# Hash attention beside an FFN on one core: the two casts of P ahead of the exponential, a hash's bits behind the gate's low part

## The chip, the core and the metric

The kernel runs as one program on one NeuronCore of a Trainium2 chip. The metric is the device time of one execution in microseconds (us); lower is better. Before the change the median of three runs is 974.77 us (974.68 to 978.98). Engines are named as in the profile: PE is TensorE, with PEld for its weight loads, DVE is VectorE, ACT is ScalarE, POOL is GpSimd, SP is SyncE, which here only issues DMAs.

## The reference

Four batches of eight heads, 768 tokens, head width 64. Each token's query and key are hashed to a six-bit bucket by the signs of six projections; a query attends only to keys of its own bucket. The result goes through a feed-forward network (FFN) with 512 inputs, 2048 hidden units and a gate. All is float32; the FFN's weights come as 64-bit floats.

```python
q_bits = (np.einsum('bhsd,dk->bhsk', q, proj) > 0).astype(np.int64)
...
mask = q_bucket[:, :, :, None] == k_bucket[:, :, None, :]
scores = scale * np.matmul(q, k.transpose(0, 1, 3, 2))
scores = np.where(mask, scores, -1000000000.0)
scores = scores - np.max(scores, axis=-1, keepdims=True)
attn = np.exp(scores)
attn = attn / (np.sum(attn, axis=-1, keepdims=True) + 1e-09)
return np.matmul(attn, v).astype(np.float32)
...
h = x @ w_in
relu6 = np.clip(h + 3.0, 0.0, 6.0)
g = h * relu6 / 6.0
return (g @ w_out).astype(np.float32)
```

## The kernel before

**Splitting.** Nearly every matrix product is made of three fp32r products: each operand is a high part (a cast on ACT) and a low part (the difference, on DVE or POOL), and the product of two low parts is left out. So each operand costs a cast and a subtraction, here called `ph` and `pl` for the attention matrix P, `gh` and `gl` for the gate's output (tiles `gb` and `ga`).

**Steps.** The attention is cut into 192 steps, six tiles of 128 queries for each of 32 heads. What a step `g` needs, in order: scores on PE (`s`, lines 387 and 389); their lowest value and a copy out of PSUM on DVE (`lowest`, line 396); the exponential on ACT, in place (line 408); P turned over; the cast and the low part of P (`split_p`, lines 475, 477 and 479); and, for each pair of steps, the product with the values on PE (`acc`, lines 500 and 513).

**The stage of the change.** From step 102 (`GT`) on the attention runs beside the FFN: `beside_ffn(k)` writes down, for each step `k`, one slice of attention and one of 16 slices of an FFN chunk of 256 tokens. The orders on PE, DVE, ACT and POOL are the orders in which this function calls things; SP's queue is ordered by the scheduler. In this stage P is turned over by a DVE transpose of 32 x 32 blocks (`flip`, line 429), one DMA to DRAM (`fd`) and four DMAs back (`move`), which end in one of two tiles, `spare` for even steps and `px` for odd ones. Flip(k+2) and move(k+1) belong to step k; a move is issued behind the next flip's write to DRAM, and only when the two casts and the two low parts of the same tile's last content are done. The casts of step k are those of P(k-1), in two halves: half 1 (its low part on POOL, line 477) and half 0 (its low part on DVE, line 479). `ph` and `pl` have two buffers each, so one pair of steps fills both, and the cast of the next pair must find them free.

**The FFN's slice.** `gemm1` (12 matmuls, line 661) gives h; `gate` is a Relu on ACT (line 683) and a multiplication on DVE (line 684); at the next step's start `split_g` casts `gh` on ACT (line 689) and subtracts `gl` on DVE (line 690); `gemm2` (lines 699, 700 and 704, the last with `gl`) runs after the next step's `gemm1`. In this stage `gh` and `gl` have one buffer, so a cast waits until the `gemm2` before it has read it. The generator `ffn` yields at stages A to D, and `go("A")` and so on in `beside_ffn` run it up to the next.

**One step's order before the change.** PE: `acc` (odd steps), `gemm1`, the hash `z` (one step in six, lines 334 to 336), `gemm2` of the last slice, the scores of step k+3. ACT: `gh`, exponential, cast of half 1, on odd steps a copy `y` of a product (line 547), Relu, cast of half 0, on some steps a scaling (line 274) or cast (line 304) of the next head's q and k. DVE: `lowest`, `gl`, `flip`, gate, `pl` of half 0, and on a hash's step `bits` (line 352, two instructions), which turns `z` into the bit rows of q, from where a DMA copies rows to k; the scores of the next head need them two steps later. On the step behind a hash `gl` stands ahead of `lowest`. `add` lets POOL issue DMAs that accumulate the second half of a head's result into DRAM (`xs`).

Of the kernel before, what the change touches and what calls it, by code (L numbers as in the profile page):

```python
# [28 lines left out]
LA = 3  # L29
# [3 lines left out]
LT = 1  # L33
# [10 lines left out]
def lsh_attention_moe(  # L44
# [10 lines left out]
    nc = tc.nc  # L55
# [3 lines left out]
    KT = S // P  # L59
# [20 lines left out]
    paced = False  # L80
# [147 lines left out]
    NS = NJ * KT  # L228
# [3 lines left out]
    GT = GF + FT  # L232
# [139 lines left out]
    scs, probs, outs = {}, {}, {}  # L372
# [110 lines left out]
    def split_lows():  # L483
        for f in lows:
            f()
        lows.clear()
# [31 lines left out]
    adds, fresh = [], []  # L518
# [10 lines left out]
    def output(un: int):  # L529
        nonlocal vdone  # L530
        i, u = divmod(un, KT // 2)
        b, h = divmod(i, H)
        o = (h % 2) * D
        acc = accs.pop(un)

        if u != 1:
            outs[i] = sp.tile([P, 4 * P if u == 0 else 2 * P], F32, name=f"y{i}_{u}", tag=f"y{u}", bufs=1)
        y = outs[i][:, 2 * P :] if u == 1 else outs[i][:, : 2 * P]

        r = slice(o, o + D)  # L540
        r2 = slice(D - o, 2 * D - o)
        last_head = h == H - 1 and u == (0 if b else 2)
        if last_head:
            nc.scalar.copy(y[r], acc[r2])
            nc.vector.tensor_add(y[r], acc[r], y[r])
        else:
            nc.scalar.copy(y, acc[:])
        if u or last_head:
            single = last_head or h == H - 1 and b
            c = slice(2 * u * P, 2 * (u + 1) * P) if single else slice(0, 4 * P) if u == 1 else slice(4 * P, S)  # L550
            to = xs[b][h * D : (h + 1) * D, c]

            with tc.issue_after(copied.ins):
                dma(out=to, in_=y[r] if single else outs[i][r])
            if not last_head:
                ts = (u,) if single or u else (0, 1)
                (fresh if single and u == 2 else adds).append((i, ts if u != 1 or single else (0, 1), to, y[r2] if single else outs[i][r2]))
        vdone = 2 * un + 2


# [118 lines left out]
    def gate(n: str, fc: int, hg, copy, engine, between=lambda: None):  # L679

        hp, g = hg[:, 0], hg[:, 1]
        r = sp.tile([P, TC], F32, name=f"g{n}_{fc}", tag="g", bufs=1)
        nc.scalar.activation(r[:], hp, AF.Relu, bias=three[:], scale=1.0)  # L683
        nc.vector.scalar_tensor_tensor(out=g, in0=r[:], scalar=6.0, in1=hp, op0=ALU.min, op1=ALU.mult)  # L684
        between()

        def split():
            gh, gl = gate_tiles(f"{n}_{fc}")
            copy(gh, g)  # L689
            engine.tensor_sub(gl, g, gh.bitcast(F32))  # L690
            return gh, gl

        return split
# [31 lines left out]


    xr0, x0 = {}, {}
    side, opening, amid = [], [], []

    def beside():  # L730
        if side:
# [195 lines left out]
    def ffn():  # L927
# [49 lines left out]
        for c, (b, t) in enumerate(chunks):  # L977
            while not there(c):
                if pend is not None:
                    finish()()  # L980
                stage = "B"
                yield
            n = f"{b}_{t}"
            if c not in xr:
                begin(c)
            while side:
                beside()
                stage = "B"
                yield
                if not paced:  # L990
                    yield
            if c not in xhl:
                place(c)
                for cc in range(NCC):
                    split(c, cc)
            ffn_on = True
            copy = nc.scalar.copy
            po = None
            for fc in range(NFC):
                hp = gemm1(n, fc, xhl[c])  # L1000
                stage = "C"
                yield
                end = finish() if pend is not None else lambda: None
                if po is None:
                    po = ps.tile([P, 2, 512], F32, name=f"po{n}", tag="s" if b == B - 1 and t % 2 == 0 else "po", bufs=1)
                parted = paced
                split_g = gate(n, fc, hp, copy, nc.vector, lambda: amid and amid.pop()())
                if not parted:
                    gg = split_g()
                end()  # L1010
                if c + 1 < len(chunks) and c + 1 not in xr and there(c + 1):
                    if fc >= XF[chunks[c + 1][0] == B - 1]:
                        begin(c + 1)
                if parted:
                    stage = "D"
                    yield
                    for _ in range(-(-len(side) // (NFC - fc))):
                        beside()
                if fc + 1 == NFC and c + 1 in xr and c + 1 not in xhl and not side:
                    place(c + 1)  # L1020
                    for cc in range(NCC):
                        split(c + 1, cc)
                elif not parted:
                    beside()
                if parted:
                    stage = "A"
                    yield
                    gg = split_g()
                pend = ((b, t), (fc, [po[:, u] for u in range(2)], *gg))
                stage = "B"  # L1030
                yield
                if not parted:
                    beside()
            del xhl[c]
# [64 lines left out]
    with tc.manual_schedule(engines={ET.PE, ET.DVE, ET.Activation, ET.Pool}):  # L1099
# [9 lines left out]
        def go(part: str):  # L1109
            if stage == part:  # L1110
                next(fill, None)
# [3 lines left out]
        def beside_ffn(k: int):  # L1115

            nonlocal paced, stage, held
            held = False  # L1120
            if k < GT:
                for c in range(2):
                    transp(k, c)
                exponential(k + 1)
            for _ in range(2):
                u = vnext // 2
                if u < NS // 2 and (2 * u < GT or k % 2 and k >= 2 * u + 3):
                    if vnext % 2 == 0 and k >= GT:
                        value_whole()
                        through.append(u)  # L1130
                        break
                    if value_half():
                        through.append(vnext // 2 - 1)
                if k < GT:
                    break
            behind = (k - 1 + LA) % KT == 4
            if GT <= k < NS - 2 and not behind:
                lowest(k + 2)
            go("A")
            if GT <= k < NS - 2 and behind:  # L1140
                lowest(k + 2)
            if k < GT:
                for c in range(2):
                    split_p(k, c, False)
                split_lows()
                while through:
                    output(through.pop(0))
                flip(k + 1)
            if k + 2 < NS:
                if k < GT:  # L1150
                    lowest(k + 2)
                    assert len(side) <= 2
                    opening.pop()()
                if k == GT:
                    go("B")
                    go("C")
                exponential(k + 2)
            paced = True
            multiply()
            if k + 2 < NS:  # L1160
                flip(k + 2)
            split = GT <= k - LT < NS
            if split:
                split_p(k - LT, 1, False)
            go("B")
            if k == NS + LT:
                homes.clear()
            while through and (through[0] < vnext // 2 - 1 or k % 2 == 0 or k < GT):
                output(through.pop(0))
            hashed = k + LA < NS and (k + LA) % KT == 4 and (k + LA) // KT + 1 < NJ  # L1170
            if hashed:
                hash_qk((k + LA) // KT + 1)
            if split:
                amid.append(lambda: (split_p(k - LT, 0, False), split_lows()))
            go("C")
            while amid:
                amid.pop()()
            split_lows()
            if hashed:
                bits((k + LA) // KT + 1)  # L1180
            if k + LA < NS:
                lead(k + LA)
            if moves:
                moves.pop(0)()
            if GT <= k + 1 < NS:
                move(k + 1)

            place_in_chunk = (k - GT) % NFC
            if subs and (k % 2 and (k < GT or place_in_chunk != NFC - 1) or k > GT and place_in_chunk == 0):
                subs.pop(0)()  # L1190
            go("D")
            if k % KT in (1, 3):
                add()
# [134 lines left out]
```

## Time and profile before

One profiled execution, which took 973.11 us; its span, from the first to the last instruction, is 971.3 us.

| | |
|---|---|
| runs shown | 974.68, 974.77, 978.98 us |
| profiled execution, and its span | 973.11 us, 971.3 us |
| PE | busy 948.0 us (98%), 6306 matmuls |
| DVE | busy 723.5 us (74%) |
| ACT | busy 625.0 us (64%) |
| POOL | busy 473.6 us (49%) |
| granted TensorE clock, mean | 0.998 |

The page's "idle before, releaser" and the view of waits name, for each idle stretch of an engine, whose semaphore ended it. A busy share of 98% does not say that PE works at its peak: its matmuls overlap and their ends are modelled, so a short wait can be hidden in it. The attention beside the FFN takes the stretch from about 405 to 815 us; ahead of it lie attention alone and the first batch's FFN, behind it the last chunks of the FFN.

### The profile page before, as it was taken

Reading aid. Unit: us, or ns where it says so; the run is one execution under the profiler, and the core shown is the slowest. Engines: PE = TensorE matmul, PEld = TensorE weight load, DVE = VectorE, ACT = ScalarE, POOL = GpSimd, SP = SyncE. Lnnn points to the kernel's source line nnn. Section 1 sums busy time; section 2 is a strip of 40 time slices with the busy share of each in tenths; the row PEclk is TensorE's granted clock in tenths of the full one; section 3 lists DMA queues with packets and bytes.
Section 4 is the critical chain, followed back from the end, with each engine's and each line's share of the span. In section 5 each row is a group of like instructions: output and inputs, shape, how many; then the busy total and the mean of one; then the engine's idle time right before and its main releaser. Section 6 shows DMA issues by size and latency. Waiting matters only on the chain.

```text
span 971.3 us, 19460 instructions
## 1 busy us (share of the span) xinstructions
PE 948.0 (98%) x6306; PEld 873.6 (90%) x6306; DVE 723.5 (74%) x1470; ACT 625.0 (64%) x1421; POOL 473.6 (49%) x582
## 2 busy tenths in 40 slices
PE   8999999999999999899999999999999999999997
PEld 7999888999989999799899899989899899889896
DVE  7999988888569999877878878878777874342422
ACT  6898875655478988667766666666666664333332
POOL 6777744665537776455555545555545432000000
PEclk9999999999999999999999999999999999999999
DMA  3567579100035554787898788788887772101000
GB/s 117 140 156 188 131 224 377 58 1 1 6 119 119 115 142 112 192 252 233 238 267 234 231 256 241 230 267 236 243 258 233 211 227 71 44 1 44 1 22 22
DMA packets 113613, 152.06 MB, mean 157 GB/s; under 512 B 13876, under 2 KB 82612, under 8 KB 113512
## 3 DMA queue, kind: packets, MB, share of 16 engines
q1 hardware_dynamic: 108472, 144.79, 48.8%
q0 software_dynamic: 5040, 6.03, 5.3%
q8 instruction: 50, 0.82, 0.4%
q14 instruction: 51, 0.42, 0.2%
HBM read 77.34 MB, written 54.00 MB: 135 GB/s over the span
## 4 chain that ended last, share of the span: by engine, by line
PE 79%; DVE 8%; DMA 4%; ACT 4%; issue 3%; POOL 1%; SPq 1%; ACTq 0%; DVEq 0%; POOLq 0%
PE h L661 25%; PE acc L500 6%; PE po L704 6%; PE po L699 6%; PE po L700 6%; PE acc L513 6%; PE pt L418 5%; PE s L389 5%; PE s L387 5%; DMA spare<-fd 2%; DVE p L396 2%; DVE pl L479 2%; ACT ph L475 1%; SPq L78 1%; DVE qq L352 1%
## 5 line engine op out<-in xcount | busy, mean ns | idle before, releaser
L408 ACT ACTIVATE p<-p,m 128x768 f32<-128x768 f32 x192 | 180.2, 939 | 113.4 <-DVE p L396 105.2
L396 DVE TENSOR_SCALAR_CACHE_REDUCE p<-s 128x768 f32<-128x768 f32 x192 | 182.7, 952 | 24.9 <-PE pt L418 12.4
L684 DVE SCALAR_TENSOR_TENSOR h<-g,h 128x256 f32<-128x256 f32 x192 | 81.1, 423 | 102.0 <-ACT g L683 99.0
L683 ACT ACTIVATE g<-h,three 128x256 f32<-128x256 f32 x192 | 91.2, 475 | 94.9 <-PE h L661 94.0
L661 PE MATMUL h<-xh,w 128*128 128x256 f32 x1024 | 146.8, 282 | 0.0
L661 PEld LDWEIGHTS h<-xh,w 128*128 128x128 f32 x1024 | 134.9, 188 | 4.2 <-ACT xh L650 0.6
L429 DVE STREAM_TRANSPOSE p<-p 128x768 f32<-128x768 f32 x90 | 88.1, 979 | 65.2 <-ACT p L408 65.1
L477 POOL TENSOR_TENSOR pl<-spare,ph 128x384 fp32r<-128x384 f32 x45 | 45.8, 1018 | 127.3 <-ACT ph L475 71.4
L479 DVE TENSOR_TENSOR pl<-pt,ph 128x384 fp32r<-128x384 f32 x196 | 100.0, 550 | 4.0 <-ACT ph L475 3.5
L387 PE MATMUL s<-kk,qq 76*128 76x384 f32 x384 | 100.5, 343 | 2.0 <-ACT kk L357 1.5
L389 PE MATMUL s<-kk,qq 128*128 128x384 f32 x384 | 100.4, 343 | 0.0
L700 PE MATMUL po<-w,gb 128*128 128x512 f32 x250 | 98.4, 393 | 0.0
L699 PE MATMUL po<-w,gb 128*128 128x512 f32 x250 | 98.3, 393 | 0.0
L475 ACT CAST ph<-pt 128x384 fp32r<-128x384 f32 x196 | 86.1, 474 | 14.3 <-PE pt L418 13.0
L216 POOL TENSOR_TENSOR w<-wr,w 128x128 fp32r<-128x128 f32 x128 | 71.9, 593 | 45.2 <-ACT w L210 41.9
L418 PE MATMUL pt<-ident,p 128*128 128x128 f32 x612 | 86.2, 275 | 1.9 <-DVE pl L479 1.1
L689 ACT CAST gb<-h 128x256 fp32r<-128x256 f32 x141 | 52.4, 372 | 54.5 <-DVE h L684 26.8
L661 PE MATMUL h<-xl,w 128*128 128x256 f32 x512 | 81.2, 280 | 0.0
L418 PEld LDWEIGHTS pt<-ident,p 128*128 128x128 f32 x612 | 72.5, 141 | 8.9 <-PE pt L418 1.5
L704 PE MATMUL po<-w,gb 128*128 128x512 f32 x250 | 78.6, 395 | 1.5 <-DVE gb L690 1.5
L318 POOL TENSOR_TENSOR kk<-raw,qq 64x192 fp32r<-64x192 f32 (+1 forms) x73 | 65.4, 920 | 25.1 <-ACT qq L304 21.7
L387 PEld LDWEIGHTS s<-kk,qq 76*128 76x128 f32 x384 | 66.6, 190 | 11.7 <-ACT kk L357 2.0
(153 smaller groups left out, 2150.9 us busy)
## 6 DMA issues: line engine op xcount, KB each, us to landing
fd<-p SPq DMA_DIRECT2D x90, 384.0 KB
spare<-fd SPq DMA_DIRECT2D x180, 96.0 KB
px<-fd SPq DMA_DIRECT2D x180, 96.0 KB
kk<-qq SPq DMA_DIRECT2D x62, 192.0 KB
wr<-in_w_in SPq DMA_DIRECT2D x16, 512.0 KB
wr<-in_w_out SPq DMA_DIRECT2D x16, 512.0 KB
raw<-in_qkT SPq DMA_DIRECT2D x19, 384.0 KB
vr<-in_v SPq DMA_DIRECT2D x32, 192.0 KB
```

The costliest lines, as they stand in the source:

```text
L387: nc.tensor.matmul(s[:, c, :HW], lhsT=q1[:KM, us], rhs=half(k1[:KM], c), start=True, stop=False)
L389: nc.tensor.matmul(s[:, c, :HW], lhsT=q2[:, us], rhs=half(k2, c), start=False, stop=True)
L396: nc.vector.tensor_scalar(out=pr_[:], in0=s[:, :, :HW], scalar1=CAP, scalar2=None, op0=ALU.min, op1=ALU.min, accum_out=m[:],)
L408: nc.scalar.activation(pr_[:], pr_[:], AF.Exp, bias=m[:], scale=-1.0, accum_out=sms[b][:, t, h : h + 1])
L418: nc.tensor.transpose(pt[:, x], probs[g][0][:, c, x * P : (x + 1) * P], ident[:])
L475: nc.scalar.copy(hi, pt)
L479: lows.append(lambda: engine.tensor_sub(lo, pt, hi.bitcast(F32)))
L661: nc.tensor.matmul(hp, lhsT=wi[:, wp, wc], rhs=x[cc][xp], start=(k == 0 and cc == 0), stop=(k == 2 and cc == NCC - 1),)
L683: nc.scalar.activation(r[:], hp, AF.Relu, bias=three[:], scale=1.0)
L699: nc.tensor.matmul(po[u], lhsT=gh[:, us], rhs=wo[:, 0], start=(fc == 0), stop=False)
L700: nc.tensor.matmul(po[u], lhsT=gh[:, us], rhs=wo[:, 1], start=False, stop=False)
L704: nc.tensor.matmul(po[u], lhsT=gl[:, us], rhs=wo[:, 0], start=False, stop=(fc == NFC - 1))
```

## The change

`split_p` is no longer called in two places (half 1 behind the flip, half 0 between the gate and the next step). A new inner function `halves_of` calls it for half 1 and half 0 and then runs the DVE low part, and it is called behind `go("A")` and ahead of the step's exponential and flip; only the first such step (k = 103) has it behind the flip. The hook `amid`, by which `gate` called half 0, is gone. A hash's `bits` are put on a list and run in the next step behind `go("A")`, that is behind `gl`; `lowest` of that step comes behind them, and behind `gl` in step 103 also. The accumulating DMA of the last third of a batch's last head is no longer held back by one call of `add` in this stage.

```diff
-                (fresh if single and u == 2 else adds).append((i, ts if u != 1 or single else (0, 1), to, y[r2] if single else outs[i][r2]))
+                (fresh if single and u == 2 and not paced else adds).append((i, ts if u != 1 or single else (0, 1), to, y[r2] if single else outs[i][r2]))
...
-                split_g = gate(n, fc, hp, copy, nc.vector, lambda: amid and amid.pop()())
+                split_g = gate(n, fc, hp, copy, nc.vector)
...
-            behind = (k - 1 + LA) % KT == 4
+            behind = bool(todo_bits) or k == GT + 1
             if GT <= k < NS - 2 and not behind:
                 lowest(k + 2)
             go("A")
+            while todo_bits:
+                bits(todo_bits.pop())
             if GT <= k < NS - 2 and behind:
                 lowest(k + 2)
+
+            def halves_of(g: int):
+                for c in (1, 0):
+                    split_p(g, c, False)
+                split_lows()
+
+            split = GT <= k - LT < NS
+            if split and k - LT > GT:
+                halves_of(k - LT)
...
             if k + 2 < NS:
                 flip(k + 2)
-            split = GT <= k - LT < NS
-            if split:
-                split_p(k - LT, 1, False)
+            if split and k - LT == GT:
+                halves_of(k - LT)
             go("B")
...
-            if split:
-                amid.append(lambda: (split_p(k - LT, 0, False), split_lows()))
             go("C")
-            while amid:
-                amid.pop()()
-            split_lows()
             if hashed:
-                bits((k + LA) // KT + 1)
+                todo_bits.append((k + LA) // KT + 1)
```

No instruction is added or taken away, and PE's order is the same row for row. On ACT, two steps (106 and 107) before the change, from the exponential on; `p` is P before its turn, `ph_1` and `ph_0` are the casts of the two halves, `g` is the Relu, `gb` is `gh`, `y` the copy of a product:

```order
L408 ACTIVATE p_5796,sms_5285<-p_5796,m_5795 128x768
L475 CAST ph_1_5748<-px 128x3x128
L547 COPY y_0_5820<-acc_5725 128x256
L683 ACTIVATE g_0_4_5828<-h_0_4_5807,three 128x256
L475 CAST ph_0_5774<-px 128x3x128
L689 CAST gb_0_4_5859<-h_0_4_5807 128x256
L408 ACTIVATE p_5857,sms_5285<-p_5857,m_5856 128x768
L475 CAST ph_1_5866<-spare 128x3x128
L683 ACTIVATE g_0_5_5893<-h_0_5_5870,three 128x256
L475 CAST ph_0_5892<-spare 128x3x128
L689 CAST gb_0_5_5913<-h_0_5_5870 128x256
```

The same two steps on ACT after the change:

```order
L475 CAST ph_1_5744<-px 128x3x128
L475 CAST ph_0_5748<-px 128x3x128
L408 ACTIVATE p_5796,sms_5285<-p_5796,m_5795 128x768
L547 COPY y_0_5822<-acc_5725 128x256
L683 ACTIVATE g_0_4_5830<-h_0_4_5809,three 128x256
L689 CAST gb_0_4_5859<-h_0_4_5809 128x256
L475 CAST ph_1_5862<-spare 128x3x128
L475 CAST ph_0_5866<-spare 128x3x128
L408 ACTIVATE p_5857,sms_5285<-p_5857,m_5856 128x768
L683 ACTIVATE g_0_5_5893<-h_0_5_5874,three 128x256
L689 CAST gb_0_5_5913<-h_0_5_5874 128x256
```

Both casts now stand between `gh` and the exponential; nothing of P is left between the exponential and the next `gh`.

On DVE, a step with a hash (109) and the head of the next before the change; `p,m` is `lowest`, `gb` is `gl`, `h` the gate, `pl` the low part, `qq<-z` the bits, the transpose is the flip:

```order
L396 TENSOR_SCALAR p_5974,m_5973<-s_5950 128x768
L690 TENSOR_TENSOR gb_0_6_5976<-h_0_6_5922,gb_0_6_5976 128x256
L429 STREAM_TRANSPOSE p_5974<-p_5974 128x768
L684 SCALAR_TENSOR_TENSOR h_0_7_5987<-g_0_7_6014,h_0_7_5987 128x256
L479 TENSOR_TENSOR pl_0_6018<-spare,ph_0_6017 128x3x128
L352 TENSOR_SCALAR qq_5779<-z_0_6000,thr,val 44x384
L352 TENSOR_SCALAR qq_5779<-z_1_6001,thr,val 44x384
L690 TENSOR_TENSOR gb_0_7_6037<-h_0_7_5987,gb_0_7_6037 128x256
L396 TENSOR_SCALAR p_6041,m_6040<-s_6027 128x768
L429 STREAM_TRANSPOSE p_6041<-p_6041 128x768
```

The same place on DVE after the change:

```order
L396 TENSOR_SCALAR p_5974,m_5973<-s_5950 128x768
L690 TENSOR_TENSOR gb_0_6_5976<-h_0_6_5924,gb_0_6_5976 128x256
L479 TENSOR_TENSOR pl_0_5984<-spare,ph_0_5983 128x3x128
L429 STREAM_TRANSPOSE p_5974<-p_5974 128x768
L684 SCALAR_TENSOR_TENSOR h_0_7_5991<-g_0_7_6018,h_0_7_5991 128x256
L690 TENSOR_TENSOR gb_0_7_6034<-h_0_7_5991,gb_0_7_6034 128x256
L352 TENSOR_SCALAR qq_5779<-z_0_6004,thr,val 44x384
L352 TENSOR_SCALAR qq_5779<-z_1_6005,thr,val 44x384
L396 TENSOR_SCALAR p_6041,m_6040<-s_6024 128x768
L479 TENSOR_TENSOR pl_0_5984<-px,ph_0_5983 128x3x128
L429 STREAM_TRANSPOSE p_6041<-p_6041 128x768
```

The low part has gone from behind the gate to ahead of the flip, and the two bits have changed places with `gl`; nothing but the gate's own cast now stands between the gate and `gl` there.

More of the change, by code (lines that the diff above doesn't have):

```diff
@@ L727, in lsh_attention_moe @@
     xr0, x0 = {}, {}
-    side, opening, amid = [], [], []
+    side, opening, todo_bits = [], [], []
     def beside():
```

## The prediction

> **What bounds the kernel now.** The page's first line gives the span; the sum row of the busy times by window for the attention beside the FFN (405 to 815 us) says how little PE can still gain there.
>
> ```profile
> span 971.3 us, 19460 instructions
> sum 410.00, PE 404.05 PEld 372.86 DVE 319.21 ACT 271.38 POOL 213.12; mean PE 101.01 PEld 93.22 DVE 79.80 ACT 67.84 POOL 53.28
> ```
>
> PE is idle for 410.00 - 404.05 = 5.95 us of 410. As no instruction goes and PE's order stays, only PE's waits can shrink. The view of waits names them, first for PE, then for its weight loads (total, times, longest, in us).
>
> ```profile
> PE acc L513 <- ACT ph L475: 4.5, 9, 1.5
> PE po L704 <- DVE gb L690: 1.5, 2, 0.8
> PEld acc L513 <- ACT ph L475: 6.0, 12, 1.7
> PEld po L704 <- DVE gb L690: 2.4, 2, 1.2
> PEld acc L513 <- issue: 2.2, 3, 0.9
> ```
>
> Two things hold PE: the product with the values waits for a cast of P, and `gemm2` waits for `gl`. A lost moment lies between the PE row (ends of matmuls are modelled and hide part of it) and the weight-load row. Lower bound of all of it 4.5 + 1.5 = 6.0 us, upper 6.0 + 2.4 + 2.2 = 10.6 us; I take 6.0 + 2.4 = 8.4 us.
>
> The other engines are not full, but wait for each other in a ring (waits of ACT, then of DVE):
>
> ```profile
> ACT p L408 <- DVE p L396: 93.2, 82, 2.9
> ACT gb L689 <- PE po L704: 24.9, 32, 1.5
> DVE p L429 <- ACT p L408: 64.4, 87, 1.1
> ```
>
> The exponential waits 93.2/82 = 1.14 us for `lowest`, the flip 0.74 us for the exponential. The 32 waits of `gh` for line 704 come from its single buffer. The timeline (start, duration) of a hash's step and the head of the next shows the ring and, beside it, PE's deadlines:
>
> ```profile
> 651.22 0.37 ACT L689 CAST gb<-h 128x256 fp32r<-128x256 f32 x1
> 651.58 0.95 DVE L396 TENSOR_SCALAR_CACHE_REDUCE p<-s 128x768 f32<-128x768 f32 x1
> 652.45 0.42 DVE L690 TENSOR_TENSOR gb<-h,gb 128x256 fp32r<-128x256 f32 x1
> 652.57 0.94 ACT L408 ACTIVATE p<-p,m 128x768 f32<-128x768 f32 x1 [0.98 <-DVE p L396]
> 653.51 0.50 ACT L475 CAST ph<-spare 128x384 fp32r<-128x384 f32 x1
> 653.63 0.98 DVE L429 STREAM_TRANSPOSE p<-p 128x768 f32<-128x768 f32 x1 [0.76 <-ACT p L408]
> 653.99 0.48 ACT L683 ACTIVATE g<-h,three 128x256 f32<-128x256 f32 x1
> 654.37 0.50 ACT L475 CAST ph<-spare 128x384 fp32r<-128x384 f32 x1
> 654.53 0.40 DVE L684 SCALAR_TENSOR_TENSOR h<-g,h 128x256 f32<-128x256 f32 x1
> 654.64 0.34 SPq L78 DMA_DIRECT2D fd<-p  x1
> 654.90 0.62 DVE L479 TENSOR_TENSOR pl<-spare,ph 128x384 fp32r<-128x384 f32 x1
> 655.55 1.29 DVE L352 TENSOR_SCALAR qq<-z,thr,val 44x384 fp32r<-44x384 f32 x2
> 655.59 1.30 SPq L78 DMA_DIRECT2D spare<-fd  x3
> 656.38 0.37 ACT L689 CAST gb<-h 128x256 fp32r<-128x256 f32 x1 [1.51 <-PE po L704]
> 656.87 0.42 DVE L690 TENSOR_TENSOR gb<-h,gb 128x256 fp32r<-128x256 f32 x1
> 657.21 0.95 DVE L396 TENSOR_SCALAR_CACHE_REDUCE p<-s 128x768 f32<-128x768 f32 x1
> 658.20 0.94 ACT L408 ACTIVATE p<-p,m 128x768 f32<-128x768 f32 x1 [1.45 <-DVE p L396]
> 659.69 0.52 PE L387 MATMUL s<-kk,qq 76*128 76x384 f32 x2
> ```
>
> **Part 1: the casts ahead of the exponential.** `gh` ends at 651.59 and ACT idles 0.98 us until 652.57. Two casts of 0.50 us fill that hole: 651.6 to 652.6, the exponential moves by 0.0 us here. The cast of half 0 ends at 652.6 instead of 654.87, 2.3 us earlier, and no longer stands behind the Relu, which waits for PE. What that is worth where PE waits is plain in the longest wait:
>
> ```profile
> 631.47 0.50 ACT L475 CAST ph<-px 128x384 fp32r<-128x384 f32 x1
> 633.07 0.37 ACT L547 COPY y<-acc 128x256 f32<-128x256 f32 x1 [1.10 <-DMA xs<-y]
> 633.70 0.51 ACT L475 CAST ph<-px 128x384 fp32r<-128x384 f32 x1
> 634.27 0.63 PE L513 MATMUL acc<-ph,vv 128*128 128x256 f32 x3 [1.50 <-ACT ph L475]
> ```
>
> A copy that waited 1.10 us for its buffer's DMA held the Relu and the cast behind it. Of casts that PE waits for (odd P, cast on even steps), each moves ahead of this: the term is -6.0 us (-4.5 to -8.2). The Relu loses one cast ahead of it, so the gate is then set by the flip, not by the Relu.
>
> The buffers of `ph` are held by the product of the pair before, which PE runs at an odd step's start; there a cast may now meet it. PE needs that cast only two steps later, and its Relu waits for the 12 matmuls behind that product anyway. Cost nothing; if the cover failed, the exponential would slip by a part of the three-matmul groups above (0.63 us) on odd steps.
>
> **Part 2: the low part ahead of the flip.** DVE idles 0.74 us there. The low part's durations against POOL's (minimum, median, maximum in ns):
>
> ```profile
> L479 DVE TENSOR_TENSOR pl<-spare,ph x45: 557/642/869, 407.0 to 808.1; 128x384 fp32r<-128x384 f32 x45
> L477 POOL TENSOR_TENSOR pl<-spare,ph x45: 1011/1018/1024, 406.4 to 806.6; 128x384 fp32r<-128x384 f32 x45
> ```
>
> Before, POOL's 1.02 us was mostly over when DVE's began; now DVE's starts 0.5 us into it. Placed in the step above: `gl` ends at 652.87, the low part lasts 0.56 to 0.87 and ends by 653.74, the flip could start at about 653.65. Cost 0 to 0.1 us a step, on a ring with room: I take 0. A rule speaks against the move: the Trainium skill, "SBUF — State Buffer", section "SBUF: two separate sides", says that a VectorE instruction with two SBUF inputs and a GpSimd instruction that reads SBUF exclude each other, the loser blocking fully. By that rule the low part would begin at POOL's end, 653.1, and end at 653.7, the same place to 0.1 us; the trace agrees in part (869 is above 557), but does not show a full block.
>
> **Part 3: the bits behind `gl`.** Before, the low part and the bits filled DVE from 654.90 to 656.84, while `gh` waited for PE until 656.38. Now `gl` is first and waits for `gh`: 656.75 + 0.02 to 657.19; then bits to 658.48; `lowest` to 659.45; the exponential at 659.5 instead of 658.20. So each hash delays the ring by 1.3 us, and there are 14 in the stage. The scores at 659.69, which overwrite what `lowest` reads, are missed by 0.2 us. Behind it every step of the ring is `gh` 0.37 + casts 1.0 + exponential to flip 1.06 + flip 0.98 + gate 0.40 = 3.8 us, so the delay is worn off within the head. The place at which it could hurt is the second `gl` behind the hash, which has little spare time before (DVE, then PE):
>
> ```profile
> 666.47 0.42 DVE L690 TENSOR_TENSOR gb<-h,gb 128x256 fp32r<-128x256 f32 x1
> 667.72 0.62 PE L704 MATMUL po<-w,gb 128*128 128x512 f32 x2
> ```
>
> 0.83 us. Following the ring from 659.5: flip to 661.6, gate to 662.0, `gh` behind a scaling of q (0.85 us) to 662.7, casts to 663.7, exponential, flip 664.8 to 665.8, gate to 666.1, `lowest` to 667.0, `gl` to 667.4: 0.3 us are left. I charge 0.3 us for a third of the 14 heads, those in which DVE also scales x: +1.4 us (0 to +7, half a microsecond in each head). The two waits for `gl` lie in the stage's first steps, the second here, behind `lowest` and the bits; `gl` now comes ahead of both: -2.4 us (-1.5 to -2.4).
>
> ```profile
> 409.61 0.73 PE L704 MATMUL po<-w,gb 128*128 128x512 f32 x2 [0.74 <-DVE gb L690]
> ```
>
> The bits' rows reach k some 1.6 us later; the scores need them a step later: nothing.
>
> **Part 4: the DMA of P.** A cast now asks for its data 2.1 us earlier in a step (exponential 0.94 plus 1.14 idle). The move is issued on SP behind the next flip's write, and the flip is now behind the low part. Two casts at the stage's end that waited for their data show the way from issue to use:
>
> ```profile
> 801.75 1.76 SPq L78 DMA_DIRECT2D spare<-fd  x4
> 806.02 0.51 ACT L475 CAST ph<-spare 128x384 fp32r<-128x384 f32 x1 [1.38 <-DMA spare<-fd]
> L408 ACT ACTIVATE p<-p,m x87: 936/938/951, 404.8 to 798.7; 128x768 f32<-128x768 f32 x87
> ```
>
> 4.27 us. From one cast to the cast two steps on: casts 1.0, exponential to flip 1.06, flip 0.98, write issued 0.03 + 0.34, move to use 4.27: 7.7 us. Two steps last 2 x (798.7 - 404.8)/86 = 9.2 us, so 1.5 us are spare, less what SP carries besides (loads of q, k, v and x; 0.3 to 1.0 us a place). Some casts will wait some tenths, ahead of the exponential and the gate; `gl`'s 0.8 us and more cover most. I charge four places of 0.3 us: +1.2 us (0 to +6).
>
> **Part 5: the accumulating DMA one call earlier.** Once in the stage: 0 to +0.8, taken as 0.
>
> **Sum.** -6.0 - 2.4 + 1.4 + 1.2 = -5.8 us on 973.11: 967.3. The profiled execution lies 1.66 us below the median of 974.77, so the forecast is 974.77 - 5.8 = 969.0 us.
>
> **The rivals.**
>
> *All of it comes.* No charge falls due and the issue waits go too: 974.77 - 10.6 = 964.2. For it: the ring's step of 3.8 us is shorter than a step of 4.6. Against: 0.3 us left behind a hash.
>
> *The waits change their owner.* PE stops waiting for casts and waits for `gl` and scores instead, by nearly the same sum: with both charges at about half of their upper ends, +3.5 + 3 = 6.5 against 8.4: 973, and up to 979 at the ends. For it: PE 98% busy, and the ring's slack of 0.8 us at best. In this case too belongs that the change does less than it says, as the casts of odd steps are held by the product of the pair before.
>
> *Slower: the hash's delay is not worn off.* In each head DVE idles from 654.93 to 656.77 and the ring loses 1.3 us. If the ring, not PE, sets the pace over the six steps, 14 x 1.3 = 18 us come on top of -8.4: 984. It decides if the ring's mean step beside this exceeds PE's, that is if casts wait for DMA in most steps (over 4.58 - 3.8 - 1.3/6 = 0.56 us a step), since then nothing is made up. For it: the ring is the longest chain beside PE, and Part 4's spare time is small. Against: the waits of 0.98 and 0.76 us in the step above, which the casts and the low part fill.
>
> **How the numbers follow.** A measurement of this kernel can tell about 0.5% (4.9 us): faster is below 969.9, slower above 979.6. Forecast's case 0.50 (965 to 973; a little over half below 969.9), all of it 0.17, waits change owner 0.17, slower 0.16. Faster: 0.33 + 0.17 = 0.50; same: 0.17 + 0.17 = 0.34; slower 0.16. The range takes the first three cases, from 963 to 978.
>
> **What would show it.** Right: in the waits, the line "PE acc <- ACT ph" is gone, and ACT's idle before the exponential falls from 1.14 us to a few tenths; the exponential behind a hash starts 3.1 us after `gh` does, against 1.8 now. Wrong towards slower: ACT's casts released by "DMA px<-fd" in dozens of steps, PE's line 704 waiting for `gl` in most heads, scores waiting for `lowest`. Wrong towards faster: none of these, and PE's idle time under 2 us in the stage.

## The result, and the profile after

The change makes the kernel slower: 982.94 us (median of 4 runs, 982.32 to 985.22) against 975.02 us (4 runs, 974.68 to 978.98) for the kernel before on the same chip, a ratio of 1.0083 with a 95% interval of [1.0062, 1.0105]. The forecast of 969.0 and its range up to 978 are both missed, on the slow side. The profiled execution took 985.22 us against 973.11 before; it is the slowest of its four runs, while the one before was quicker than all of its own, so the two profiles lie further apart (12 us) than the medians (7.9 us).

The profile after has a span of 983.4 us against 971.3. The sum row of the busy times in the attention beside the FFN, which now ends some 10 us later (405 to 825 us):

```profile
sum 420.00, PE 400.01 PEld 367.96 DVE 343.99 ACT 273.52 POOL 212.58; mean PE 400.01 PEld 367.96 DVE 343.99 ACT 273.52 POOL 212.58
```

PE idles 420.00 - 400.01 = 20.0 us where it idled 5.95 before: 14 us more, beside a span that is 12.1 us longer. So the loss is again to be read from PE's waits alone. The view of waits for PE after the change (total, times, longest):

```profile
PE h L661 <- DVE qq L352: 10.3, 10, 1.1
PE rt L587 <- DVE qq L352: 3.0, 3, 1.0
PE po L699 <- ACT gb L689: 3.0, 3, 1.5
PE rt L587 <- DVE xr L590: 1.2, 1, 1.2
PE s L387 <- DVE p L396: 1.1, 1, 1.1
PE acc L513 <- POOL pl L477: 0.8, 2, 0.4
PE po L704 <- DVE gb L690: 0.3, 1, 0.3
```

Both waits that the prediction wanted gone have all but left the view: `acc` no longer waits for a cast, and line 704 waits 0.3 us for `gl`. But at the stage's first steps, where line 704 had waited 0.80 and 0.74 us for `gl`, PE now waits longer for two others, `gh` and the scores behind `lowest`:

```profile
408.66 0.50 PE L699 MATMUL po<-w,gb 128*128 128x512 f32 x1 [1.50 <-ACT gb L689]
411.44 0.62 PE L387 MATMUL s<-kk,qq 76*128 76x384 f32 x2 [1.11 <-DVE p L396]
```

And a wait that stood in no view before has come: PE's first matmul behind a hash, `gemm1` (line 661) or a transposition of x (line 587), waits for the bits (`qq`, line 352), 13 times, 13.3 us. In this trace that is about the whole difference of the two spans; what the bits cost in time is measured further down.

The waits of ACT and DVE, to be held against the 93.2 us and 64.4 us shown before:

```profile
ACT ph L475 <- DMA px<-fd: 33.5, 31, 2.3
ACT p L408 <- DVE p L396: 21.5, 20, 2.0
ACT ph L475 <- DMA spare<-fd: 7.5, 7, 2.0
DVE p L429 <- ACT p L408: 7.2, 16, 1.1
```

The casts fill the hole ahead of the exponential, as meant. But in 38 steps they wait for P's way through DRAM, 41.0 us in all, where two did before.

The timeline of a hash's step and the next one's head (start, duration; in brackets the idle time before and what ended it):

```profile
491.26 0.63 PE L704 MATMUL po<-w,gb 128*128 128x512 f32 x2
491.93 0.37 ACT L689 CAST gb<-h 128x256 fp32r<-128x256 f32 x1 [1.27 <-PE po L704]
492.09 0.52 PE L389 MATMUL s<-kk,qq 128*128 128x384 f32 x2
492.33 0.42 DVE L690 TENSOR_TENSOR gb<-h,gb 128x256 fp32r<-128x256 f32 x1 [0.66 <-ACT gb L689]
492.79 1.29 DVE L352 TENSOR_SCALAR qq<-z,thr,val 44x384 fp32r<-44x384 f32 x2
493.36 0.93 ACT L475 CAST ph<-px 128x384 fp32r<-128x384 f32 x2 [1.06 <-DMA px<-fd]
493.62 1.18 PE L661 MATMUL h<-xh,w 128*128 128x256 f32 x8 [1.01 <-DVE qq L352]
494.11 0.96 DVE L396 TENSOR_SCALAR_CACHE_REDUCE p<-s 128x768 f32<-128x768 f32 x1
495.11 0.94 ACT L408 ACTIVATE p<-p,m 128x768 f32<-128x768 f32 x1 [0.83 <-DVE p L396]
```

Read it as a chain: line 704 ends, `gh` gets its buffer, `gl` follows `gh`, the bits follow `gl`, and `gemm1` starts when the first of the two bits' instructions is done (the row of 1.29 us is two, 0.69 us each on the median), 1.01 us after PE ran out of scores. Line 704 is queued on PE between the hash and that `gemm1`, so the work that the bits now wait for has used up all the time that they had. In the kernel before, the bits of the step shown in the prediction end at 656.84, and this is the matmul behind them:

```profile
656.90 1.10 PE L661 MATMUL h<-xh,w 128*128 128x256 f32 x8
```

It starts at 656.90, with no idle time. The first of the two bits' instructions had ended at about 656.2 (655.55 + 0.69), so there were only some 0.7 us to spare. Nothing in a view of waits shows a wait that has not yet come.

Why `gemm1` needs the bits at all is not in the code's operands but in PSUM, PE's output memory, which is divided into banks. `bank` (line 93) deals out four of them to `z`, `h`, `acc` and `rt`. The built program, with the bank of each half of `z` and then the tiles that PE fills behind it:

```
z19 [6, 5]   h 6, acc 4, h 7
z20 [5, 7]   rt 5, h 6, rt 5, acc 7, h 4
z21 [7, 4]   h 7, acc 5, h 6
z22 [5, 6]   h 5, acc 7, h 4
```

Behind 13 of the stage's 14 hashes the next tile takes the bank of the first half of `z`, and may be written only when the bits have read it; behind the stage's first hash it takes another, and no wait stands there. In the program of the kernel before it is the same 13.

### The profile page after: what moved, and what is told of

The parts are those of the page before. It is cut to its first block, busy times and chain, and to the rows that moved or that the text cites. A ratio compares the mean times of both kernels' runs of the same rounds, so it can differ in the third digit from the quotient of the medians.

```text
span 983.4 us, 19468 instructions
## 1 busy us (share of the span) xinstructions
PE 945.9 (96%) x6306; PEld 870.3 (88%) x6306; DVE 748.7 (76%) x1470; ACT 627.8 (64%) x1421; POOL 473.0 (48%) x582
## 4 chain that ended last, share of the span: by engine, by line
PE 72%; DVE 10%; DMA 5%; SPq 4%; issue 3%; ACT 3%; POOL 2%; DVEq 0%; ACTq 0%; POOLq 0%
PE h L661 23%; PE acc L500 6%; PE po L704 6%; PE po L699 6%; PE po L700 6%; PE pt L418 5%; PE s L389 4%; SPq L78 4%; PE s L387 4%; PE acc L513 4%; DMA px<-fd 4%; DVE pl L479 3%; DVE p L396 2%; DVE qq L352 2%; ACT ph L475 1%
## 5 line engine op out<-in xcount | busy, mean ns | idle before, releaser
L475 ACT CAST ph<-pt 128x384 fp32r<-128x384 f32 x196 | 85.9, 473 | 14.6 <-PE pt L418 13.3
L690 DVE TENSOR_TENSOR gb<-h,gb 128x256 fp32r<-128x256 f32 x141 | 59.1, 419 | 26.7 <-ACT gb L689 26.4
```

The source lines that it names most:

```text
L475: nc.scalar.copy(hi, pt)
```

## The experiments

The theory after these views: two new waits make the loss. The bits hold PE through the shared bank, and the casts, asked for earlier, wait for P's DMA. The rivals: the ring of ACT and DVE has become the bound and sets the pace whatever PE waits for, which was the slower rival of the prediction; or the low part on DVE, slower beside POOL's, is to blame. Each kernel ran beside the kernel before on the same chip, and its ratio is to that.

### Half of the change at a time

The casts alone: the whole change with the bits back at the end of their own step and `lowest` in its old place.

```diff
-            behind = bool(todo_bits) or k == GT + 1
+            behind = (k - 1 + LA) % KT == 4
...
-            while todo_bits:
-                bits(todo_bits.pop())
...
-                todo_bits.append((k + LA) // KT + 1)
+                bits((k + LA) // KT + 1)
```

> The changed kernel with the hash's bits put back at the end of their own step; the casts and the low part stay ahead of the exponential and the flip. Theory A (PSUM bank: the first matmul behind a hash writes into the bank of z's first half, so PE waits for the bits wherever they stand): the 14 waits of about 1.2 us, 16.9 us in all, go, 983 - 17 = 966 us, 966 to 969. Theory B (VectorE's ring loses 1.3 us a head): the same, 966 to 970. Theory C (casts wait for P's DMA and hold ScalarE): no change, 980 to 984.

Measured: 977.88 us, 1.0028 [1.0013, 1.0042]. Its waits:

```profile
ACT ph L475 <- DMA px<-fd: 33.8, 33, 2.6
ACT ph L475 <- DMA spare<-fd: 15.2, 16, 2.5
PE po L699 <- ACT gb L689: 3.3, 5, 1.3
PE acc L513 <- POOL pl L477: 2.7, 7, 0.7
```

The casts alone are no gain but a small loss, so the bits are not the whole cause: they explain 1.0083 - 1.0028 = 0.0055, or 5.4 us of 8. The casts wait for DMA in 49 steps, 49.0 us; PE meets that as waits for `gh` and for POOL's low part.

The bits alone, on the kernel before:

```diff
-            behind = (k - 1 + LA) % KT == 4
+            behind = bool(todo_bits)
...
             go("A")
+            while todo_bits:
+                bits(todo_bits.pop())
...
-                bits((k + LA) // KT + 1)
+                todo_bits.append((k + LA) // KT + 1)
```

> The kernel before with only the bits moved to the next step behind gl; casts and low parts stay in their old places. Theory A: 14 waits of about 1.2 us appear on PE in front of the next h, 975 + 14 to 17 = 989 to 992 us, less what the bits' place saves at the start (up to 1 us). Theory B: the ring loses up to 1.3 us a head, 980 to 992, with gl or the scores, not h, as PE's wait. Theory C: 975 us, no change.

Measured: 988.95 us, 1.0135 [1.0116, 1.0154], the dearest half, with this line among PE's waits:

```profile
PE h L661 <- DVE qq L352: 11.9, 10, 2.0
```

The halves don't add up: 0.0028 + 0.0135 = 0.0163 against 0.0083 for both. The two kinds of wait overlap: while PE waits for the bits, P's DMA goes on, and the casts' waits for it are 41.0 us in the whole change against 49.0 with the casts alone. That this overlap is all of the difference is argued, not shown.

### Is it the bank?

The whole change, with the turn of the banks moved on by one behind the hash, so that the next tile takes neither bank of `z`:

```diff
             z = zs[i] = [bank([P, HW], f"z{i}_{j}") for j in range(2)]
+            turn += 1
```

> The changed kernel with one turn of the PSUM banks skipped behind a hash in this stage, so that the next h or transpose is written into a bank that the gate, not the bits, has read; the order on every engine is the same. Theory A: PE's waits for the bits go, 966 to 969 us. Theory B: nothing changes, 982 us, since VectorE still loses its 1.3 us a head. Theory C: 982 us.

Measured: 980.92 us, 1.0056 [1.0038, 1.0074], far from what I expected. The wait for the bits goes but for three of 0.3 us, but the tile now takes the bank of the `h` before, which `gl` releases (lines of the kernels with another turn are two further down):

```profile
PE h L663 <- DVE gb L692: 5.4, 11, 3.3
```

One of these waits, 3.3 us, stands at the stage's start, where the turn is moved too. The rest are 0.2 us each. The bank is a cause, but moving it brings back 0.0083 - 0.0056 = 0.0027, or 2.6 us: the casts still wait, and the new wait at the stage's start may take its part.

### Is it the DMA?

In the casts-only version the casts and the low parts read a constant tile in place of P, so that the product is not computed from P; all DMAs still run, but no cast waits for one.

```diff
-            pt = moved[g].rearrange("p (i x a) -> p x i a", i=4, x=KT)[:, c * QT : (c + 1) * QT]
+            pt = ident[:].rearrange("p (i a) -> p i a", i=4).unsqueeze(1).to_broadcast([P, QT, 4, P // 4])
```

> The kernel with the casts alone moved (bits in their old place), in which the casts and low parts of this stage read a constant tile instead of P turned over; the four DMAs back are still issued, in the same place, but nobody waits for them and they wait for no cast. So the product with the values is not computed from P. Theory D (the casts ahead of the exponential wait for P's DMA, 49 us in all on ScalarE, and this comes back as PE's waits for gh, gl and POOL's low part): 978 - 11 = 967 us, 965 to 969. Theory R (the casts make the ring itself longer, with or without the DMA): 975 to 978.

Measured: 966.85 us, 0.9919 [0.9904, 0.9934]. That is 7.9 us below the kernel before, for casts and low part alone: `lowest` of step 103 is in its old place here, and PE's waits for `gl` are still there. And it gives the price of the DMA waits in the casts-only version: 1.0028 - 0.9919 = 0.0109, or 10.6 us. The first of PE's waits that are left:

```profile
PE po L704 <- DVE gb L690: 1.7, 2, 1.5
PE acc L513 <- POOL pl L477: 0.7, 1, 0.7
```

The same tile in the whole change:

> The changed kernel with the same constant tile in place of P turned over. Theories A and D together: the DMA's part goes and the 14 waits for the bits stay, 967 + 14 to 17 = 981 to 984 us if nothing else takes them in, so hardly below the changed kernel. Theory D alone (the DMA is all of the loss): 967. Theory R: 983.

Measured: 978.87 us, 1.0039 [1.0027, 1.0052]; beside the version above on the same chip, so with no DMA wait the bits cost 978.87 - 966.85 = 12.0 us. In the whole change the DMA waits are worth less than in the casts alone: 1.0083 - 1.0039 = 0.0044, or 4.3 us. The bits' line is unchanged, 13 waits and 13.2 us with the three of line 587:

```profile
PE h L661 <- DVE qq L352: 10.1, 10, 1.0
```

And in the kernel before, as a control:

> The kernel before with the constant tile in place of P turned over (so the product with the values is not computed from P): a control for what the constant tile alone brings. Theory D: the casts hardly waited for DMA in the kernel before, so 973 to 975 us. If the tile itself makes things faster (theory T: fewer waits for the moves, other bytes), 967 to 970.

Measured: 974.13 us, 0.9991 [0.9979, 1.0003]: no difference that can be told (0.9 us), so the constant tile by itself explains little, and before the change the DMA of P was no burden.

Then the bank and the constant tile together: the whole change, the turn moved on behind each hash but the stage's first, and casts and low parts that read the constant tile (the product is not computed from P).

```diff
-            turn += 1
+            turn += i > GT // KT + 1
```

> The changed kernel with the constant tile and with the turn of PSUM banks skipped behind each hash but the first, so that the next h or transpose waits for gl and not for the bits. Theory A (bank): of the 13 waits of 1.2 us about 0.36 each is left, 979 - 13 x 0.8 = 969 us, 967 to 972. Theory B (VectorE's ring loses 1.3 us a head): 977 to 980, as without the skip.

Measured: 971.98 us, 0.9961 [0.9949, 0.9973], inside the range of the bank theory and below that of the ring. Of the 0.0120 that the bits cost without DMA waits, 1.0039 - 0.9961 = 0.0078 is the bank; 0.0042, or 4.1 us, is left. In it PE's ten waits are down to 0.2 us each, and the three places with a transposition have two waits of 0.3 us:

```profile
PE h L663 <- DVE gb L692: 2.0, 10, 0.2
PE rt L589 <- DVE gb L692: 0.9, 3, 0.3
PE h L663 <- DVE qq L354: 0.9, 3, 0.3
```

In those three the `h` behind the transposition gets the bank of `z` after all, by the built program. The three rows sum to 3.8 us, which would cover most of the 4.1 us left, so the trace gives no sign that the ring of ACT and DVE takes a share of the bits' price; that it takes none is not shown.

### Can the DMA be had earlier, or the casts later?

The kernel with the other bank, and P's DMAs back of the next step written ahead of the flip, from the third step of the stage on:

```diff
+            ahead_of_flip = k > GT + 1
+            if ahead_of_flip and GT <= k + 1 < NS:
+                move(k + 1)
...
-            if GT <= k + 1 < NS:
+            if not ahead_of_flip and GT <= k + 1 < NS:
                 move(k + 1)
```

> The kernel of the other bank with P's four DMAs back from DRAM written down ahead of the flip and so issued ahead of the next flip's write. Theory A: the casts' waits for DMA shrink, PE hardly gains, within 2 us of the kernel of the other bank. Theory C: the casts' waits of 41 us in all on ScalarE fall by more than half and the time by 5 us or more against it.

Measured: 1009.48 us, 1.035 [1.033, 1.037], the worst of all. SP's queue in its timeline, and DVE:

```profile
499.82 0.98 DVE L431 STREAM_TRANSPOSE p<-p 128x768 f32<-128x768 f32 x1 [0.51 <-ACT p L410]
...
502.07 1.86 SPq L78 DMA_DIRECT2D px<-fd  x4
504.04 0.38 SPq L78 DMA_DIRECT2D fd<-p  x1
...
507.81 0.96 DVE L398 TENSOR_SCALAR_CACHE_REDUCE p<-s 128x768 f32<-128x768 f32 x1 [1.49 <-DMA fd<-p]
```

A flip that ends at 500.80 has its write to DRAM issued at 504.04, behind the four reads of 502.07. `lowest` needs the buffer of P that this write reads, and waits 1.49 us. In all:

```profile
DVE p L398 <- DMA fd<-p: 46.1, 34, 3.5
PE po L706 <- DVE gb L692: 13.6, 16, 2.5
```

SP's own waits say why:

```profile
SPq L78 <- DMA fd<-p: 85.1, 60, 4.7
```

Written down earlier, the reads wait on SP in 60 places until the write that they read has landed (85.1 us in all, against 1.5 us in the kernel of the other bank), and the next write, which frees a buffer of P, stands behind them.

Now the casts later: both right behind the exponential, where their data had been in time, the low part of half 0 behind the flip and ahead of the gate, the bits in their old place.

```diff
-            if split and k - LT > GT:
-                halves_of(k - LT)
...
-            if split and k - LT == GT:
+            if split:
                 halves_of(k - LT)
```

> The bits in their old place, both casts right behind the exponential (instead of ahead of it), the low part on VectorE behind the flip and ahead of the gate. The casts ask for their data 1.1 to 2 us later. Theory D: ScalarE's waits for P's DMA fall below 15 us, PE's waits for casts stay away, 969 to 973 us. Theory R: the low part ahead of the gate lengthens the ring, 975 to 980.

Measured: 985.07 us, 1.0104 [1.0091, 1.0118]. The DMA waits are nearly gone (4.8 us), yet it is slower than the casts-only version:

```profile
ACT ph L475 <- DMA px<-fd: 2.8, 3, 1.2
ACT p L408 <- DVE p L396: 73.0, 84, 3.5
PE acc L513 <- ACT ph L475: 3.1, 7, 0.8
PEld acc L513 <- POOL pl L477: 8.7, 25, 0.8
```

The low part, 1.0 us, stands ahead of the gate, and `gh` now waits for the gate 51.2 us in 62 steps, where it waited 2.1 us before the change; the exponential has its hole again, and PE's waits for casts, which were to stay away, are back with 3.1 of their 4.5 us. The missing DMA waits alone are no gain if the ring pays for them.

The same on even steps alone, on the kernel before (half 0 at once behind half 1, odd steps as they were):

```diff
                 split_p(k - LT, 1, False)
+                if k % 2 == 0:
+                    split_p(k - LT, 0, False)
+                    split_lows()
...
-            if split:
+            if split and k % 2:
                 amid.append(lambda: (split_p(k - LT, 0, False), split_lows()))
```

> The kernel before, in which on even steps alone (whose casts PE needs at the next step's start) half 0 follows half 1 at once, with its low part ahead of the gate; odd steps and the bits as before. Theory D: PE's waits for casts go for the most part, no new ones for DMA, 969 to 973 us. Theory R: 974 to 977.

Measured: 979.0 us, 1.0042 [1.003, 1.0055]: 0.4 of the loss above, for half of the steps.

And the change's own place, ahead of the exponential, on even steps alone (those whose casts PE had waited for), on the kernel before (the calls in the old places stay for the other steps):

```diff
+            first = split and k - LT > GT and k % 2 == 0
+            if first:
+                for c in (1, 0):
+                    split_p(k - LT, c, False)
+                split_lows()
```

> The kernel before, in which on even steps alone both casts stand ahead of the exponential and the low part ahead of the flip; odd steps and the bits as before. Theory D: the product's waits for casts go, the casts wait for DMA in about half as many steps as with all of them moved, 974 to 976 us. Theory R (the ring's length): as the ring is not longer on even steps and as before on odd ones, 969 to 972.

Measured: 976.28 us, 1.0004 [0.9989, 1.002], no difference. PE's waits for casts went (0.2 us are left), but waits for POOL's low part came (3.3 us), and the casts of these steps alone wait for DMA nearly as much as those of all:

```profile
ACT ph L475 <- DMA px<-fd: 43.4, 37, 3.1
```

### The slower low part

The casts-only version with half 0 first, so that DVE's low part starts half a microsecond ahead of POOL's instead of behind it:

```diff
             def halves_of(g: int):
-                for c in (1, 0):
+                for c in (0, 1):
```

> The kernel with the casts alone moved, in which half 0 (low part on VectorE) is cast ahead of half 1 (low part on GpSimd), so that VectorE's low part starts first. Theory L (the two low parts shut each other out, and the second one waits for the first to end): VectorE's low part falls from 1.07 us to about 0.56 us, and GpSimd's, which then starts as VectorE's ends, stays at 1.02. On the time: if VectorE's low part lay on the ring's critical way, 88 x 0.5 us would show, 978 down to 960 or less; if it is hidden in the wait for the exponential, as the sum of the prediction had it, 975 to 980. If the longer low part has another cause (theory M: place in the order), it stays near 1.07.

Measured: 975.44 us, 0.9996 [0.9983, 1.001]. The low part's durations (minimum, median, maximum in ns):

```profile
L479 DVE TENSOR_TENSOR pl<-spare,ph x45: 516/557/1405, 407.6 to 808.4; 128x384 fp32r<-128x384 f32 x45
```

And the flip's waits for the exponential, from the view of waits:

```profile
DVE p L429 <- ACT p L408: 45.3, 73, 0.8
```

557 ns again, and the flip waits for the exponential in 73 steps, not for the low part. Worked out from all flips of the timeline, it starts on the mean 1.10 us behind the exponential's start; 1.19 with half 1 first, 1.06 before the change. The time falls by 0.0032, about 3 us. Whether that is the low part's own price is asked of three more kernels.

The whole change with half 0 first:

> The whole change with half 0 first in place of half 1. Theory L: the low part takes 0.56 instead of 1.07 us, the flip starts 0.1 us earlier in a step, and about 3 us of the change's 8 us come back: 978.5 to 981 (1.0035 to 1.006). Rival N: 982 to 984 (1.007 to 1.009), since PE still waits for the bits and the casts for P's DMA.

Measured: 984.31 us, 1.0096 [1.0081, 1.0111]. The low part is at 557 ns here too, and nothing comes back: PE still waits 13.2 us for the bits.

Even steps alone, ahead of the exponential as in the last kernel of the group above, with half 0 first:

> The kernel before with both casts and VectorE's low part ahead of the exponential and the flip on even steps alone, half 0 first. With half 1 first this gave 1.0004 [0.9989, 1.002] of before. Theory L (VectorE's low part, begun while GpSimd's runs, costs the ring what it is longer): its duration on even steps falls from 1.07 to 0.56 us and half of the 3 us comes back, 972.5 to 975 (0.9975 to 1.0). Rival N (the slower low part lies beside other work and costs nothing): 975 to 978, as with half 1 first.

Measured: 975.82 us, 1.0004 [0.9992, 1.0015]: the same as with half 1 first, though the low part of these steps fell from 1060 to 559 ns on the median. (PE's waits for casts are back with 3.6 us.)

Casts only, constant tile (the product is not computed from P), half 0 first:

> The casts alone, half 0 first, and the casts and low parts read a constant tile in place of P, so that the product isn't computed from P. With half 1 first this gave 966.85 (0.9919). Theory L with the ring as the bound even here: 963 to 965 (0.988 to 0.990). Rival: once the DMA is not waited for PE sets the pace, and the shorter low part is worth nothing: 966 to 968 (0.991 to 0.993).

Measured: 964.35 us, 0.9892 [0.9877, 0.9906], 2.6 us below the version with half 1 first by the ratios. But its low part took 844 ns on the median, so the gain is not put to the 0.5 us alone.

So two pairs show about 3 us (in the second of them the intervals just touch) and two show none: the order of the halves is worth up to 3 us where the bits hold nobody up, and nothing in the whole change. Whether the low part's own length makes it stays open. No version that computes P's product beats the kernel before.

## Why the prediction was wrong

**Part 1, the casts ahead of the exponential (-6.0): right.** The row "PE acc <- ACT ph" is gone, ACT's wait for `lowest` fell from 93.2 to 21.5 us, and without DMA waits and with the bits in their old place the kernel takes 0.9919 of its time: -7.9 us, within the range of -4.5 to -8.2. "Cost nothing" for the buffers of `ph` was nearly so: seven casts wait for the product, 3.5 us in all on ACT.

**Part 2, the low part ahead of the flip (0): the rule was stronger than I let it be.** Durations after:

```profile
L479 DVE TENSOR_TENSOR pl<-spare,ph x45: 1030/1067/1122, 406.8 to 818.7; 128x384 fp32r<-128x384 f32 x45
```

One place on POOL and DVE, from the timeline after:

```profile
489.02 1.03 POOL L477 TENSOR_TENSOR pl<-spare,ph 128x384 fp32r<-128x384 f32 x1 [2.66 <-ACT ph L475]
489.39 1.07 DVE L479 TENSOR_TENSOR pl<-spare,ph 128x384 fp32r<-128x384 f32 x1 [0.20 <-ACT ph L475]
```

I gave it 0.56 to 0.87 us and said that the trace shows no full block. DVE's low part now takes 1.07 us: it begins 0.37 us into POOL's and ends 0.41 us behind it, as if it did nearly all of its 0.56 us afterwards. That the loser of the two blocks fully is what the Trainium skill says in "SBUF — State Buffer", section "SBUF: two separate sides"; the trace after agrees to about 0.15 us (0.41 beside 0.56). The sum hardly depended on it: the flip was to start at the same place to 0.1 us, and it starts on the mean 1.22 us behind the exponential's start, not 1.06. "On a ring with room" is the doubtful part: with the casts alone the order of the halves moved the time by 3 us.

**Part 3, the bits behind `gl` (+1.4): failed.** The prediction followed the bits' delay along the ring of ACT and DVE, got the exponential right (3.1 us behind `gh`'s start; 495.11 - 491.93 = 3.18) and looked for its victim a step later, at the second `gl` and the scores. PE had already paid, at the first matmul behind the hash, through a PSUM bank that it shares with `z`: 13.3 us in the trace, 12.0 us measured without DMA waits, 5.4 us on top of the casts. The step that failed is its list of who needs the bits: it named the scores, and left out who needs the memory that the bits read.

**The first `gl` (-2.4, in Part 3): did not come.** Line 704's two waits at the stage's start, 0.80 and 0.74 us, went as forecast, but 1.50 us for `gh` and 1.11 us for the scores stand in their place: the low part of step 103 now stands ahead of the gate, and the bits of the stage's first hash ahead of `lowest`. From line 699's first matmul of step 103 (403.31 us in the timeline after, 403.18 before) to those scores (411.44 and 410.48) PE takes 8.13 us, where it took 7.30.

**Part 4, P's DMA (+1.2): mis-sized.** "Four places of 0.3 us" were 38 places of 1.1 us. By the constant tile they cost 4.3 us in the whole change, and 10.6 us in the casts-only version, where they are 49: nearly four times the term, and nearly nine times. The mechanism was named and the loop written down; its terms were taken from places at the stage's end where SP had little else to issue. The loop's DMA part at one of the busier places after the change:

```profile
477.22 0.98 DVE L429 STREAM_TRANSPOSE p<-p 128x768 f32<-128x768 f32 x1 [0.30 <-ACT p L408]
478.22 0.39 SPq L78 DMA_DIRECT2D fd<-p  x1
478.72 0.41 SPq L78 DMA_DIRECT2D out<-ob  x1
479.22 3.03 SPq L78 DMA_DIRECT2D px<-fd  x4
484.69 0.93 ACT L475 CAST ph<-px 128x384 fp32r<-128x384 f32 x2 [1.85 <-DMA px<-fd]
```

From write to move 1.00 us where I took 0.34, since an output's store stands between; the four moves take 3.03 us to issue where the sampled place took 1.76; and 5.47 us from issue to use where I took 4.27. That is 1.9 us above the sum of 7.7, and the 1.5 us that I had to spare are gone. Over all 38 waiting casts the way from issue to use is 5.1 us on the median (4.1 the shortest), 0.8 above what I took, which alone would not use up 1.5 us; what takes the rest at a common place is open. I had named "0.3 to 1.0 us a place" for SP's other loads and then charged four places only.

**Part 5 (0):** no wait at the accumulating DMA appears in PE's view; no run tested it.

**The rivals.** The slower one gave 984 and came within 1.1 us, but that is luck, for its mechanism is another. It held that the ring sets the pace and nothing is made up. Its condition, 0.56 us a step for DMA, was nearly met (41.0 us in about 90 steps, 0.46), but with no DMA wait at all the bits still cost 12.0 us, and 0.0078 of 0.0120 goes when the bank alone is changed. So two thirds of their price is shown to be PE's own wait, and PE's rows left in that kernel, 3.8 us at the same tiles, would cover most of the last third.

By ratios of the kernel's time, with the parts put on in this order: casts -0.0081, DMA waits +0.0109, bits on top +0.0055, together +0.0083. What stays open is how the waits share the time where they meet: the bits cost 13 us alone, 12 without DMA waits, 5 beside them.

## What to carry to other kernels

Before a reader of a buffer is moved later, list who writes that buffer next, in PSUM too: the wait runs through memory, so neither the operands nor the waits before the change show it; the gap between the reader's end and the next writer's start (here about 0.7 us) does. A transfer's time from issue to use is to be taken from the busiest places of its queue, not from the two that happened to wait. And of two halves of a change that overlap in time, neither's price alone says what it adds to the other: run both alone and together.

## What was unexpected in the chip

VectorE's subtraction of 128 x 384 elements (rows of `spare`, medians) takes 1067 ns when GpSimd's begins 0.4 us ahead of it; GpSimd's own stays at 1.02 us. With VectorE first it takes 557 ns, about what it took ahead of this stage (549 ns), and GpSimd's takes 1.05 us in the casts-only version and 1.12 us in the whole change, so it matters who begins.
